# An attention block's third output product inside the attention loop, early splits of the first pair's operands, and a reordered first step

## The chip, the cores and the metric

One core of a Trainium2 chip runs the whole kernel. The time is device microseconds of one execution; before the change three runs gave a median of 809.31 us (808.28 to 810.48).

## What is computed

A transformer block on x of 2048 rows and 512 columns, cut here to what matters. The 2048 rows are four segments of 512 (s = 0 to 3); there are 32 heads of 16.

```python
h = layernorm(x) * (1 + ca) + sa
q, k, v = h @ wq, h @ wk, h @ wv
for s in range(4):                       # per head
    p = softmax(q[s] @ k[s].T / 4 + causal)
    o[s] = g * mem_read(q[s]) + (1 - g) * (p @ v[s])
x = x + ga * (o @ wo)                    # the output products, one per segment
h = layernorm(x) * (1 + cb) + sb
x = x + gb * (gelu(h @ w1 + b1) @ w2 + b2)
```

## The kernel before, in words

Each large product is made of three fp32r matmuls: operands are split into a high and a low part (a rounded copy, then a subtract), and high x high, high x low and low x high are summed in PSUM.

**Stages.** First come q, k, v and the memory reads. Then the attention loop runs over P = 0 to 63, a pair of heads each; two P are a group Q, four P a unit U (8 heads, one slice g of a segment's o). S parts (L609) compute scores for the row maximum, which DVE takes (L616); the maxima go through a small transpose into `ms` on ACT (L129) and by a DMA into rows 96 to 98 of qst; T parts (L698) recompute the scores transposed with the maximum inside, ACT takes the exponential (L713, L724), POOL masks (L701), and PE multiplies by V (L738) into one bank `pv`, in a loop four P behind S. `pv_out` stores through ts to TD; `pv_in` reads the denominators dn and the products opk back; `den` (L773) stores reciprocals to RD, `rb_in` reads them back as rbB; `mix` (L787, L789), `o_hi` (oh) and `o_lo` (ol, L804) follow.

**What sets the order.** Two tables in PRM: 'order' lays S, T and the slots c0 to c9 within a P, and the other entries give positions (10 x P + slot) for everything else. DVE, ACT, POOL and PE each run in the order of the code, and so does SP, which issues nearly all DMAs. Each DMA on SP waits there for what it needs.

**Output products.** `wo_part(s, b, g)` (L815) adds slice g to rows b (128 of them) of segment s: three matmuls, so 12 for a block b and 48 for a segment. `wo_out` (L832) adds x and stores to X2D. Segments 0 and 1 do this inside the loop, in the bank `mm`, one block per group, at positions PRM['wo']; segments 2 and 3 do it after the loop, in the banks that the attention has left.

**The second half** runs in pairs of segments, p = 0 for segments 0 and 1, p = 1 for 2 and 3. `ln2_load`, `ln2_stats` (L564), `ln2_rstd` (crs, L150), `ln2_apply` (L571) and `ln2_turn` (transposes L577, hr L579) make hr. Seven operands, b11, b21, t1, t2, t3, t4 and b22, are hr tiles or differences of them (`r_sub`), split by `r_hi` and `r_lo` into R. A step `quad(n)` multiplies each by its part of w1 (six matmuls, `prod`, L1036), collects in the banks X, Y and V_, and stores gelu results s to GD; fourteen steps, seven per p. Products t4 and b22 of a step run inside the next one (`c21`, `c12`). Weights are loaded as `wa` (L839), combined as wb (`w_sub`), and split by `w_hi` (L1022) and `w_lo` (L1026). `bg(n, i, ...)` hangs work behind point i of step n. After seven steps the second product with w2 (L1320) follows.

Between loop and steps stands a hand-written stretch: the 48 matmuls of segment 2, four at a time around the transposes of segment 1, then segment 3's 48, with all splits of the first step's operands woven in, and what is left of units 14 and 15 called by `rest`.

Of the kernel before, what the change touches and what calls it, by code (L numbers as in the profile page):

```python
# [12 lines left out]
ALU = mybir.AluOpType  # L13
# [10 lines left out]
VROW = 560  # L24
# [26 lines left out]
 'wo': [[2, 10, 10, 10], [6, 10, 11, 11]],  # L51
 'woout': [10, 11],
# [4 lines left out]
 'ln': [[312, 339, 374, 408], [590, 618, 630, 636]],  # L57
# [26 lines left out]
 'wout': ['vvvv', 'vava', 'vvvv'],  # L84
# [5 lines left out]
 'wsub': [642, 650],  # L90
# [13 lines left out]
def block_kernel(ctx: ExitStack, tc: tile.TileContext, x, wq, wk, wv, wo, betaq, betam,  # L104
# [88 lines left out]
    vstack = ExitStack()  # L193
    vp = vstack.enter_context(tc.tile_pool(name="vp", bufs=1, side="right"))
    V = [vp.tile([128, VROW], F32, name=f"V{b}") for b in range(NB)]
# [355 lines left out]
    def ln2_load(s, tiles=None):  # L551
        if tiles:
            xt2[s] = tiles
            for b in range(4):
                sp.dma_start(tiles[b], X2D[s][:, b, :])
        else:
            t = ce.tile([128, 4, D], F32, tag="xt2", name=f"xt2_{s}")
            xt2[s] = [t[:, b, :] for b in range(4)]
            sp.dma_start(t, X2D[s])
# [27 lines left out]
    with ExitStack() as pb:  # L587
# [208 lines left out]
        def o_hi(U):  # L796
            oh = so.tile([128, 512], F32R, tag="oh", bufs=7, name=f"oh{U}")
            copy(PRM["ohe"], oh, opks[U])
            OHL[U] = oh

        def o_lo(U):
            ol = so.tile([128, 512], F32R, tag="ol", bufs=7, name=f"ol{U}")
# [6 lines left out]
        def wo_part(s, b, g):  # L809
            if g == 0 and s < 2:  # L810
# [9 lines left out]
        def wo_x(s, b):  # L820
            xbs[s, b] = so.tile([128, D], F32, tag="xb", bufs=4, name=f"xb{s}_{b}")
# [30 lines left out]

        NP = 64
# [8 lines left out]
        def wo_load(k):  # L862
            wors[k] = so.tile([128, D], F32, tag="xb", bufs=4, name=f"wor{k}")
# [51 lines left out]
        for s in range(NSEG - 1):  # L915
            for b in range(4):
                e = 160 * s + 230 + 20 * b
                ap(e + PRM["wox"][s], wo_x, s, b)
                if s < 2:
# [19 lines left out]
        for i, (ln, ld) in enumerate(zip(PRM["ln"], PRM["lnd"])):  # L939
            ap(ln[0], ln2_load, i)  # L940
            for b in range(4):
                ap(ln[1] + ld[0] * b, ln2_stats, i, b)
# [24 lines left out]
    vstack.close()  # L967

# [10 lines left out]
    with ExitStack() as pc:  # L979
        c1 = pc.enter_context(tc.tile_pool(name="c1", bufs=1, side="right", reuse_waits="tile"))  # L980
        pf = pc.enter_context(tc.tile_pool(name="psF", bufs=1, space=PSUM, reuse_waits="tile"))
        spare = pf.tile([128, 512], F32, name="spare")
        bx, by, bv = [[pf.tile([128, 512], F32, name=f"{n}{i}") for i in range(2)] for n in ("bx", "by", "bv")]
        PROD = ("b11", "b21", "t2", "t1", "t3", "t4", "b22")

        R = {n: [[c1.tile([128, 512], F32R, name=f"r{n}{i}{k}") for k in range(2)] for i in "hl"] for n in PROD}
# [4 lines left out]

        def hk(p, n):
            a, b = 2 * p, 2 * p + 1
# [409 lines left out]
```

## Time and profile before

| what | value |
|---|---|
| median of three runs | 809.31 us |
| the profiled execution | 810.6 us, span 808.9 us |
| PE busy | 782.7 us, 97% |
| DVE, ACT, POOL busy | 69%, 58%, 40% |
| mean granted PE clock | 0.996 |
| PE busy from 460 to 480 us, the end of the attention loop | 13.04 of 20 us, clock 0.90 |
| masked maxima (L616), 384 | 192.5 us on DVE, 553 ns each |
| exponentials (L713), 256 | 125.9 us on ACT, 557 ns each |

Busy time is what an engine's instructions span. Matmuls overlap one another, so a busy PE says only that one is always under way; how fast they follow is read from their starts. The number in square brackets behind a row of the timeline is the idle time of that engine ahead of it, with what ended it.

### The profile page before, as it was taken

The page shows a single profiled execution, that of the slowest core. Times are in us where ns is not written, and L with a number is a line of the kernel's source. Part 1 is how long each engine was busy: PE and PEld are TensorE (multiplying, and loading weights), DVE is VectorE, ACT ScalarE, POOL GpSimd, SP SyncE. Part 2 cuts the span into 40 slices and gives each one's busy share as a digit, 9 for nine tenths or more (in the row PEclk, how much of TensorE's full clock was granted, in tenths as well). Part 3 has the DMA queues.
Part 4 walks back from the last instruction along what each step waited for, and adds up shares of the span by engine and source line. Part 5 has one row for each costly group of instructions (what it writes and reads, how often), then busy time and mean ns, then how long its engine had stood idle before and what let it go on. Part 6 is the DMA issues. An engine that isn't in the chain of part 4 may idle for free.

```text
span 808.9 us, 14151 instructions
## 1 busy us (share of the span) xinstructions
PE 782.7 (97%) x4585; PEld 531.5 (66%) x4585; DVE 555.5 (69%) x1413; ACT 467.2 (58%) x914; POOL 327.0 (40%) x550
## 2 busy tenths in 40 slices
PE   8999999999999999999999879999999999999998
PEld 4877777866444455445544338778877888888886
DVE  6686697459888877896688567976668766532423
ACT  3465545465778766776688755677644336653221
POOL 1357366441478555677866641234000404300000
PEclk9999999999999999999999989999999999999999
DMA  9596857495565676766667744764665634445443
GB/s 336 176 315 230 290 182 234 146 339 154 154 192 171 177 199 175 220 212 189 185 182 205 213 132 132 243 206 137 221 233 183 200 127 155 158 143 169 158 135 112
DMA packets 107523, 156.10 MB, mean 193 GB/s; under 512 B 16181, under 2 KB 55477, under 8 KB 107065
## 3 DMA queue, kind: packets, MB, share of 16 engines
q1 hardware_dynamic: 104952, 153.23, 59.5%
q10 hardware_dynamic: 2496, 1.97, 0.8%
q8 instruction: 36, 0.59, 0.3%
q14 instruction: 39, 0.31, 0.1%
HBM read 93.95 MB, written 60.83 MB: 191 GB/s over the span
## 4 chain that ended last, share of the span: by engine, by line
PE 73%; DVE 7%; DMA 7%; ACT 5%; issue 3%; POOL 3%; SPq 1%; ACTq 0%; DVEq 0%; POOLq 0%
PE bx L1036 8%; PE pv L738 7%; PE att L698 6%; PE att L609 5%; PE q L315 5%; PE bx L1320 4%; PE k L315 4%; PE bv L1036 4%; PE by L1320 4%; PE bv L1320 4%; PE v L466 3%; PE mm L815 2%; PE spare L1320 2%; PE by L1036 2%; DMA RD<-dn 1%
## 5 line engine op out<-in xcount | busy, mean ns | idle before, releaser
L616 DVE CUSTOM_DVE_ANT_0 dump<-att,maskb 128x512 bf16<-128x512 f32 (+2 forms) x384 | 192.5, 553 | 22.5 <-PE att L609 19.8
L713 ACT ACTIVATE pt<-att 128x512 f32<-128x512 f32 (+1 forms) x256 | 125.9, 557 | 42.2 <-PE att L698 40.9
L701 POOL TENSOR_SCALAR_AFFINE_SELECT pt<-pt 128x256 f32<-128x256 f32 x256 | 100.9, 411 | 79.7 <-ACT pt L713 48.0
L698 PE MATMUL att<-qst,kst 99*128 99x512 bf16 (+3 forms) x512 | 107.9, 302 | 9.2 <-DMA qst<-ms 4.0
L609 PE MATMUL att<-kst,qst 96*128 96x512 bf16 (+2 forms) x384 | 94.2, 326 | 0.7 <-DVE nm L616 0.2
L851 POOL TENSOR_TENSOR wb<-wa 128x256 f32<-128x256 f32 x24 | 22.8, 950 | 162.6 <-DMA wa<-in_w 162.6
L738 PE MATMUL pv<-pt,V 128*32 128x512 f32 (+2 forms) x992 | 88.1, 446 | 0.0
L698 PEld LDWEIGHTS <-kst 99*128 99x128 bf16 x512 | 43.2, 97 | 62.1 <-issue 41.6
L138 DVE TENSOR_TENSOR gl<-s,gh 128x512 fp32r<-128x512 f32 x52 | 36.7, 706 | 66.9 <-ACT gh L135 66.9
L135 ACT ACTIVATE gh<-s 128x512 fp32r<-128x512 f32 x52 | 32.4, 629 | 74.8 <-PE spare L1320 31.7
L724 ACT ACTIVATE pt<-att 128x512 f32<-128x512 f32 (+1 forms) x128 | 56.9, 509 | 21.7 <-PE att L609 19.6
L609 PEld LDWEIGHTS <-qst 96*128 96x128 bf16 x384 | 33.1, 98 | 39.7 <-issue 23.8
L738 PEld LDWEIGHTS pv<-pt,V 128*32 128x32 f32 x992 | 22.1, 108 | 36.3 <-issue 25.7
L1041 ACT ACTIVATE s<-s,b1t 128x512 f32<-128x512 f32 x42 | 30.3, 721 | 20.1 <-DVE s L1045 19.9
L620 DVE TENSOR_REDUCE nm<-att 128x2 f32<-128x256 f32 x64 | 27.2, 426 | 21.0 <-PE att L656 18.5
L1045 DVE TENSOR_TENSOR s<-bv,s 128x512 f32<-128x512 f32 x28 | 19.2, 687 | 29.4 <-PE bv L1036 25.0
L616 DVE DVE_READ_ACCUMULATOR2_ANT nm<- 128x1 f32 x384 | 32.0, 83 | 0.0
L511 POOL TENSOR_TENSOR q<-qr,q 128x512 bf16<-128x512 f32 x16 | 18.6, 1165 | 27.9 <-ACT q L510 27.6
L502 POOL TENSOR_SCALAR qp<-qp 128x512 f32<-128x512 f32 x12 | 19.2, 1598 | 24.0 <-ACT qp L497 24.0
L1320 PE MATMUL bx<-w2h,gl 128*128 128x512 f32 (+1 forms) x70 | 26.6, 380 | 0.5 <-DVE gl L138 0.5
L1320 PE MATMUL bx<-w2h,gh 128*128 128x512 f32 (+1 forms) x70 | 26.0, 372 | 0.6 <-ACT gh L135 0.6
L315 PE MATMUL q<-Ahh,wqh 128*128 128x512 f32 x64 | 25.9, 405 | 0.2 <-DVE Ahh L137 0.2
(329 smaller groups left out, 2044.3 us busy)
## 6 DMA issues: line engine op xcount, KB each, us to landing
GD<-s SPq DMA_DIRECT2D x56, 256.0 KB
s<-GD SPq DMA_DIRECT2D x52, 256.0 KB
kst<-KD SPq DMA_DIRECT2D x32, 384.0 KB
qst<-QD SPq DMA_DIRECT2D x32, 384.0 KB
TD<-ts SPq DMA_DIRECT2D x32, 256.0 KB
wa<-in_w SPq DMA_DIRECT2D x28, 256.0 KB
QD<-q SPq DMA_DIRECT2D x16, 384.0 KB
KD<-k SPq DMA_DIRECT2D x16, 384.0 KB
```

What stands on the lines that cost most here:

```text
L135: act.activation(hi, src, AF.Copy)
L138: lo_eng.tensor_tensor(out=lo, in0=src, in1=hi.bitcast(F32), op=ALU.subtract)
L315: pe.matmul(ps, a[:, k, 128 * g:128 * g + 128], b[k], start=(k == 0 and i == 0), stop=(k == KB - 1 and i == 2))
L609: pe.matmul(ps, q_of(P, h, i), k_of(P, h, 128 * (i + 1)), start=True, stop=True)
L616: v.tensor_tensor_reduce(out=dump[n_dump[0] % 2][:, :n], in0=src, in1=maskb[:, 512 - n:], scale=-1.0, scalar=-4 * NEG, op0=ALU.add, op1=AL ...
L698: pe.matmul(ps, k[:99, e, 128 * j:128 * j + 128], q[:99, e, 128 * j:512], start=True, stop=True)
L701: pool.affine_select(out=t, in_=t, pattern=pattern, compare_op=ALU.is_ge, fill=0.0, base=0, channel_multiplier=-1)
L713: act.activation(pt[:, h, :], ps[:, :n], AF.Exp, scale=0.25)
L724: act.activation(pt, pv_, AF.Exp, scale=0.25)
L738: pe.matmul(ps[32 * c:32 * c + 32, lo:hi], V[4 * s + j][:, VW * hd:VW * hd + 32], pt[:, c % 2, lo - o:hi - o], start=start, stop=stop)
L1036: pe.matmul(ps, a[:, i, k, :], b[k], start=start and k == 0 and c == 0, stop=k == 1 and c == 2, skip_group_check=not start)
L1320: pe.matmul(ps, a[:, c], w[:, lo:hi], start=(f == 0 and i == 0), stop=(last and i == 2))
```

## The change

1. Segment 2's output product goes into the loop like the first two, at positions 552 to 621 (P = 55 to 62), in the bank `mm`; its blocks 1 and 3 leave through ACT and POOL, 0 and 2 through DVE. The two tags oh and ol keep 5 buffers, not 7, xb 3, not 4.
2. Segment 1's layernorm is loaded as four DMAs from P = 54 on, not as one at P = 59; its statistics come from 604 on, not 618, crs at 626, the application at 632.
3. The first pair's b11 and b21 are split inside the loop (positions 605 to 622) with DVE for both parts. Their tiles, and those of t1 and t3, take the storage of V tiles that are no longer read; V's rows grow from 560 to 576, and its pool stays open to the end.
4. After the loop the transposes of segment 1 come first, in the banks bx, then 24 matmuls of segment 3 (units 12 and 13), then the first step. Unit 14's 12 matmuls come behind the step's t2 product, unit 15's 12 inside the second step, with `close_wo`. In the first step t1's product runs ahead of t2's. t2 is formed as b22 - t1 in two tiles of its own, so b22 stays and is split later; t3, t4, b22's low part and two of the weights' low parts move into the step.
5. Y uses one bank per pair, not two in turn; segment 3's X2D is loaded in step 2, not 1. The ring gx has 4 tiles, not 6; every third pair of g parts goes to two weight tiles instead.

```diff
-VROW = 560
+VROW = 576
- 'wo': [[2, 10, 10, 10], [6, 10, 11, 11]],
- 'woout': [10, 11],
+ 'wo': [[2, 10, 10, 10], [6, 10, 11, 11], [2, 10, 10, 11]],
+ 'woout': [10, 11, 11],
- 'ln': [[312, 339, 374, 408], [590, 618, 630, 636]],
+ 'ln': [[312, 339, 374, 408], [548, 604, 626, 632]],
+ 'lnl': 15,
- 'wout': ['vvvv', 'vava', 'vvvv'],
+ 'wout': ['vvvv', 'vava', 'vava'],
- 'wsub': [642, 650],
+ 'wsub': [646, 652],
+ 'early': [605, 618],
...
+        RAW = {"t1": "b11", "t2": "b22", "t3": "b12", "t4": "b21"}
+        T2 = []
+        def raw(p, n):
+            return T2 if n == "t2" and p == 0 else hk(p, RAW.get(n, n))
...
+        def r_alloc(n, pl=None):
+            R[n] = [[pl.tile([128, 512], F32R, name=f"r{n}{i}{k}") if pl else
+                     vp.tile([128, VROW], F32R, tag="V", bufs=NB, name=f"r{n}{i}{k}")[:, :512] for k in range(2)]
+                    for i in "hl"]
...
+        for n, d in zip(("b11", "b21"), PRM["early"]):
+            ap(d, r_alloc, n)
+            ap(d, r_hi, 0, n, "v")
+            ap(d + 4, r_lo, 0, n)
...
-            X, Y, V_, t2 = bx[n % 2], by[n % 2], bv[n % 2], s2[n % 2]
+            X, Y, V_, t2 = bx[n % 2], by[n // FH], bv[n % 2], s2[n % 2]
...
+            if n == 0:
+                prod(n, "t1", V_, True)
...
+        for i in range(KB):
+            ln2_turn(1, i, bx[i % 2])
+            if i < 2:
+                w_hi(0, i)
+                w_lo(0, i)
+            if i == 1:
+                r_sub(0, "t1")
         for b in range(4):
             wo_seg(3, b, range(2))
...
-        bg(0, 1, ln2_load, 2)
-        bg(0, 2, close_wo)
-        bg(0, 4, r_sub, 0, "t4")
+        bg(0, 1, r_hi, 0, "t3")
+        bg(0, 2, r_lo, 0, "t3")
+        bg(0, 2, r_sub, 0, "t4")
+        bg(0, 3, wo_late, 2, 3)
+        bg(0, 3, r_lo, 0, "b22")
+        bg(0, 4, late_o)
         bg(0, 5, r_hi, 0, "t4")
         bg(0, 6, r_lo, 0, "t4")
+        for i in range(2, 4):
+            bg(0, 6, w_lo, 0, i)
+        bg(0, 6, ln2_load, 2)
+        bg(1, 2, close_wo)
```

Line numbers shift by a few in the changed kernel: output matmuls are L816, scores L699, transposes L578, the steps' matmuls L1057, w_lo L1047.

PE at the start of P = 62, before: the last scores of P = 61 (tiles kst_1838), then directly the first of P = 62 (kst_2076), which read the row maxima.

```order
L698 LDWEIGHTS kst_1838
L698 MATMUL att_2064<-qst_1837,kst_1838 128x128
L698 LDWEIGHTS kst_2076
L698 MATMUL att_2065<-qst_2075,kst_2076 128x512
L698 LDWEIGHTS kst_2076
L698 MATMUL att_2066<-qst_2075,kst_2076 128x512
```

The same place in the changed kernel, where the tiles of P = 61 and 62 are kst_2076 and kst_2139; woh and wol are the parts of wo, oh and ol those of o.

```order
L699 MATMUL att_2064<-qst_2075,kst_2076 128x128
L816 MATMUL mm<-woh,oh_4972 128x512
L816 MATMUL mm<-woh,ol_4974 128x512
L816 MATMUL mm<-wol,oh_4972 128x512
L816 MATMUL mm<-woh,oh_5209 128x512
L816 MATMUL mm<-woh,ol_5211 128x512
L816 MATMUL mm<-wol,oh_5209 128x512
L816 MATMUL mm<-woh,oh_5454 128x512
L816 MATMUL mm<-woh,ol_5456 128x512
L816 MATMUL mm<-wol,oh_5454 128x512
L699 LDWEIGHTS kst_2139
L699 MATMUL att_2065<-qst_2138,kst_2139 128x512
```

Nine matmuls of segment 2's last block stand between the two, in the bank mm.

PE right after the last product with V (into att_2065), before: segment 2's first block, with its twelve matmuls, then one group of transposes.

```order
L738 MATMUL att_2065<-pt_2_5847,V_209 32x256 x2
L738 MATMUL att_2065<-pt_2_5889,V_209 32x256 x2
L815 MATMUL bx_5953<-woh,oh_4713 128x512
L815 MATMUL bx_5953<-woh,ol_4715 128x512
L815 MATMUL bx_5953<-wol,oh_4713 128x512
L815 MATMUL bx_5953<-woh,oh_4969 128x512
```

The same place in the changed kernel: four groups of transposes in turn into two banks, then segment 3's first block.

```order
L739 MATMUL att_2065<-pt_2_5931,V_209 32x256 x2
L739 MATMUL att_2065<-pt_2_5973,V_209 32x256 x2
L578 MATMUL bx_6054<-ident,xt_1_5431 128x128 x4
L578 MATMUL bx_6055<-ident,xt_1_5431 128x128 x4
L578 MATMUL bx_6054<-ident,xt_1_5431 128x128 x4
L578 MATMUL bx_6055<-ident,xt_1_5431 128x128 x4
L816 MATMUL bv_6059<-woh,oh_5723 128x512
L816 MATMUL bv_6059<-woh,ol_5768 128x512
```

The 48 matmuls of segment 2 that stood here are gone, and the transposes, which stood one group behind each twelve of them, now follow one another.

DVE ahead of the first step's t4 product, before: w1tl are low parts of the weights that t4 and b22 use (w1tl_5992 in the first step), rt3l and rt4l low parts of the operands, xb the fourth output product's adds; the low part of t4 comes nine rows further on.

```order
L1010 TENSOR_TENSOR rt1l_5973<-hr_0_5028,rt1h_5971 128x512
L1010 TENSOR_TENSOR rt1l_5974<-hr_1_5145,rt1h_5972 128x512
L1026 TENSOR_TENSOR w1tl_5992<-wa_5608,w1th_5991 128x256
L1026 TENSOR_TENSOR w1tl_5992<-wb_5904,w1th_5991 128x256
L1010 TENSOR_TENSOR rt3l_5977<-hr_0_6028,rt3h_5975 128x512
L1010 TENSOR_TENSOR rt3l_5978<-hr_1_6057,rt3h_5976 128x512
L1045 TENSOR_TENSOR s_5995<-by_5955,s_5995 128x512
L1026 TENSOR_TENSOR w1ml_5990<-wa_5731,w1mh_5989 128x512
L832 TENSOR_TENSOR xb_0_6093<-bx_5954,xb_0_6093 128x512
```

DVE ahead of the same product in the changed kernel: opk and ol belong to unit 15, w1tl_6065 is the first step's.

```order
L887 TENSOR_TENSOR rb22l_6051<-hr_2_6103,rb22h_6049 128x512
L887 TENSOR_TENSOR rb22l_6052<-hr_3_6109,rb22h_6050 128x512
L1047 TENSOR_TENSOR w1ml_6063<-wb_6009,w1mh_6062 128x768
L788 TENSOR_TENSOR opk_6075<-opk_6075,rbB_6153 128x512
L790 TENSOR_TENSOR opk_6075<-opk_6075,amB_6077 128x512
L805 TENSOR_TENSOR ol_6233<-opk_6075,oh_6231 128x512
L1047 TENSOR_TENSOR w1tl_6067<-wa_5770,w1th_6066 128x256
L1047 TENSOR_TENSOR w1tl_6067<-wb_6009,w1th_6066 128x256
L887 TENSOR_TENSOR rt4l_6047<-hr_2_5268,rt4h_6045 128x512
L887 TENSOR_TENSOR rt4l_6048<-hr_3_5387,rt4h_6046 128x512
L1047 TENSOR_TENSOR w1tl_6065<-wa_5632,w1th_6064 128x256
L1047 TENSOR_TENSOR w1tl_6065<-wb_5995,w1th_6064 128x256
```

The first step's w1tl stood ahead of the low part of t3 and now stand behind t4's; unit 15's mix and split, which ran ahead of the first step, stand ahead of t4's low part, and the four xb adds come six rows after the last row shown. The SP load of the third step's weights, wa_6186, is issued in the code at point 1 of the first step in both kernels, ahead of its first store to GD; it overwrites wa_5632, which the first of the two w1tl_6065 rows reads.

More of the change, by code (lines that the diff above doesn't have):

```diff
@@ L191, in block_kernel @@
                        base=0, channel_multiplier=-1)
-    vstack = ExitStack()
-    vp = vstack.enter_context(tc.tile_pool(name="vp", bufs=1, side="right"))
-    V = [vp.tile([128, VROW], F32, name=f"V{b}") for b in range(NB)]
+    vstack = ctx
+    vp = vstack.enter_context(tc.tile_pool(name="vp", bufs=1, side="right", reuse_waits="tile"))
+    V = [vp.tile([128, VROW], F32, tag="V", bufs=NB, name=f"V{b}") for b in range(NB)]
     hstack = ExitStack()
@@ L1152, in block_kernel, with late_o, wo_late @@
         r_sub(0, "t3")
[L1153 to L1166 removed]
+        for b in range(4):
+            wo_x(3, b)
+        def late_o():
+            rest(15, "mem_mix", "mix", "o_hi", "o_lo")
+            assert not left, left
+        def wo_late(lo, hi):
+            for b in range(4):
+                wo_seg(3, b, range(lo, hi))
         def close_wo():
+            wo_late(3, 4)
             for b in range(4):
```

131 lines of the change are left out of this document (49 added, 82 removed).

## The prediction, made before the changed kernel had run

> **What bounds the kernel now.** I read the page's shares first, then twenty-microsecond windows. TensorE (PE) is busy in 97% of the span, and the chain of work that ended last is 73% PE.
>
> ```profile
> PE 782.7 (97%) x4585; PEld 531.5 (66%) x4585; DVE 555.5 (69%) x1413; ACT 467.2 (58%) x914; POOL 327.0 (40%) x550
> ...
> PE 73%; DVE 7%; DMA 7%; ACT 5%; issue 3%; POOL 3%; SPq 1%; ACTq 0%; DVEq 0%; POOLq 0%
> ```
>
> The windows (stretch, its length, busy time of PE, PEld, DVE, ACT, POOL, granted clock, DMA share, GB/s) show one hole: the end of the attention stage.
>
> ```profile
> 420.00:440.00 20.00, 20.00 (x183) 9.73 (x180) 17.76 (x67) 16.72 (x38) 14.21 (x29) 1.00 0.67 193
> ...
> 460.00:480.00 20.00, 13.04 (x106) 4.44 (x102) 7.19 (x15) 12.40 (x29) 12.50 (x24) 0.90 0.63 192
> ```
>
> In the full stretches more PE work means more time; in the hole it is free. So the question is how many of the 48 moved matmuls (third product, four blocks of 12) land in the hole. The hole also has two stretches at half clock, each behind a PE gap:
>
> ```profile
> 465.00:469.00 4.00, 1.06 (x13) 0.42 (x6) 1.64 (x4) 2.75 (x7) 1.97 (x6) 1.00 0.65 203
> 469.00:472.40 3.40, 3.40 (x14) 0.70 (x13) 0.00 (x0) 1.50 (x4) 0.41 (x1) 0.51 0.41 125
> ...
> 477.00:479.00 2.00, 0.00 (x0) 0.00 (x0) 0.88 (x2) 0.84 (x3) 1.97 (x4) 1.00 0.87 282
> 479.40:482.60 3.20, 3.20 (x26) 1.55 (x20) 3.13 (x7) 0.00 (x0) 1.96 (x3) 0.50 0.22 70
> ```
>
> The chain in order of time tells why the last attention products come at 479: a small store (RD) and its read-back (rbB) hold a mix on VectorE (DVE), which is first in first out; the layernorm statistics behind it come late, the crs pair on GpSimd (POOL) later still, and the last masks (L701) wait behind crs.
>
> ```profile
> 462.09 6.81 DMA RD<-dn
> 468.96 3.93 DMA rbB<-RD
> 473.01 0.87 DVE opk L787
> ...
> 476.38 0.58 POOL crs L150
> 477.03 1.05 POOL crs L151
> 478.08 0.93 POOL pt L701 x2
> 479.06 4.04 PE att L738 x22
> ```
>
> **Term 1, blocks inside the full loop: +5.4 us.** The loop runs over 64 pairs of heads; ScalarE (ACT) copies ms once per group of two pairs, so these rows count groups.
>
> ```profile
> 287.39 0.27 ACT L129 ACTIVATE ms<-mm 48x128 bf16<-48x128 f32 x1
> ...
> 329.05 0.27 ACT L129 ACTIVATE ms<-mm 48x128 bf16<-48x128 f32 x1
> ...
> 404.33 0.26 ACT L129 ACTIVATE ms<-mm 48x128 bf16<-48x128 f32 x1
> ...
> 436.41 0.27 ACT L129 ACTIVATE ms<-mm 48x128 bf16<-48x128 f32 x1
> ```
>
> Four groups with an output block each took 41.66 us (287.39 to 329.05), 10.4 a group; four without took 32.08, 8.0 a group. A block of 12 costs 2.4 us there. In the change the first two blocks (pairs 55 to 58) and three matmuls of the third (pair 59) stand in that region: 2 x 2.4 + 0.6 = 5.4. One matmul of this kind takes 0.227 us from start to start, 42 of them from 497.38 to 506.92:
>
> ```profile
> 497.38 0.39 PE L815 MATMUL by<-woh,oh 128*128 128x512 f32 x1
> ...
> 506.92 0.39 PE L1036 MATMUL bx<-rb11h,w1mh 128*128 128x512 f32 x1
> ```
>
> So the ends are 0 (all hidden, against the rows) and 27 x 0.227 = 6.1 plus the copies of one block, about 8; I take 5.4, which rows of the same work show.
>
> **Term 2, the hole: -5.0 us.** The other 21 matmuls (4.8 us) stand in pairs 60 to 62, nine of them right ahead of pair 62's first scores, where PE now waits for the DMA of ms:
>
> ```profile
> 462.47 0.23 PE L677 MATMUL mm<-identb,nm 128*128 128x128 bf16 x1 [1.59 <-POOL nm L672]
> ...
> 468.84 1.19 PE L698 MATMUL att<-qst,kst 99*128 99x512 bf16 x3 [2.94 <-DMA qst<-ms]
> ```
>
> They fill 1.59 and 2.94, so I cost them at nothing: pair 62 starts at 468.7 as now, but without the 2.94 gap ahead of it. If that cover goes (ms landing sooner), they cost up to 2 us and the landing gives it back. From there ACT sets the pace:
>
> ```profile
> 469.38 1.47 ACT L713 ACTIVATE pt<-att 128x512 f32<-128x512 f32 x3 [1.64 <-PE att L698]
> 472.36 0.49 ACT L713 ACTIVATE pt<-att 128x384 f32<-128x384 f32 x1 [1.51 <-PE att L698]
> ...
> 476.95 0.90 ACT L724 ACTIVATE pt<-att 128x512 f32<-128x512 f32 x2
> ```
>
> At full clock its 1.51 stall goes, with the 0.60 for oh further on: last exponential at about 475.7 instead of 477.85. The statistics now stand ahead of the mix, so crs comes before pair 62's last masks, not before pair 63's. Last mask about 476.4, last product 477.3 to 479; I take 478.0 against 483.03, minus 5.0. What is late next is ACT. Ends: 0 (the DMA as late and both cuts back) and -6.5.
>
> New in the hole is DVE work: four casts and four subtracts of the early split, put at 0.6 each, 4.8 us, in a stretch where DVE is busy 7.19 of 20. Queued behind them are three of the statistics, the mix and, on its result, oh on ACT; by the RD rows the mix waits till 468 or later anyway, so nothing. Two queues get a wait: SP's store of the third block waits for DVE's add ahead of RD, and the last block's for POOL's add ahead of the dn read; both adds run before the next DMA would issue now (462.09 and, by the chain of dn behind rbB, after 468.96).
>
> [...]
>
> ```profile
> 480.94 1.27 POOL L794 TENSOR_TENSOR amB<-amB,rm 128x512 f32<-128x512 f32 x1 [0.85 <-DMA rm<-rdd]
> ...
> 481.12 1.12 DVE L774 TENSOR_SCALAR dn<-dn,omg 128x32 f32<-128x32 f32 x1
> ...
> 490.27 0.24 DVE L774 TENSOR_SCALAR dn<-dn,omg 128x32 f32<-128x32 f32 x1
> ```
>
> If the eight splits hold up POOL's masks so that half of their 4.8 us shows, term 2 is -2.6.
>
> **Term 3, from the last attention product to the end of the first step: -8.6 us.** Before, from 483.03 to the end of the first step's t4 product is 37.1 us, with PE waiting 1.78 at t4:
>
> ```profile
> 517.95 0.50 PE L1036 MATMUL bx<-rt4h,w1th 128*128 128x512 f32 x1 [1.33 <-ACT s L1096]
> ...
> 519.14 0.50 PE L1036 MATMUL bx<-rt4l,w1th 128*128 128x512 f32 x1 [0.45 <-DVE rt4l L1010]
> ```
>
> After, PE's own work up to t4 with all 48 matmuls of the fourth output product is 10.9, eight products of six 10.9, transposes 1.5: 23.3. But PE waits. The third and fourth transposes need ACT's hr of the first and second, with the w_hi copies between (0.68, 0.52, 0.68 from start to start): 1.7 us.
>
> ```profile
> 486.55 0.78 ACT L579 ACTIVATE hr<-mm,cols 128x512 f32<-128x512 f32 x1 [1.72 <-PE mm L577]
> 487.23 0.62 ACT L1022 ACTIVATE w1mh<-wa 128x512 fp32r<-128x512 f32 x1
> 487.75 0.83 ACT L1022 ACTIVATE w1mh<-wb 128x768 fp32r<-128x768 f32 x1
> ```
>
> And DVE, not PE, sets t4. It was busy 31.04 us up to t4's low part; a 128x512 operation takes 0.60 from start to start:
>
> ```profile
> 483.03:519.14 36.11, 31.04 (x52) 1.00 0.55 182
> ...
> 491.29 0.68 DVE L832 TENSOR_TENSOR xb<-bx,xb 128x512 f32<-128x512 f32 x1
> 491.89 0.68 DVE L804 TENSOR_TENSOR ol<-opk,oh 128x512 fp32r<-128x512 f32 x1
> 492.49 1.29 DVE L1010 TENSOR_TENSOR rb21l<-hr,rb21h 128x512 fp32r<-128x512 f32 x2
> ```
>
> In the new order stand 18 subtracts (t1, t2, t3, t4, and the low parts of t1, t2, t3, t4, b22), two mixes of two, two ol, one add and two w_lo of that size, 27 x 0.60 = 16.2; two 768-wide w_lo, 1.8; four quarter w_lo, 1.4; den, 0.6: 20.0. It starts 2.0 after the last attention product (ts, hr, w_hi on ACT first), and waits for the second w_hi 0.9, for both oh copies 0.8 and for ACT's copies in the step 0.9: t4's low weights at 24.6, its end 25.8. The 2.7 of the last twelve output matmuls, now behind t4, still have to run: 28.5, against 37.1. Ends: 25.0 if DVE keeps up, 34 if DVE needs as long as the 31.04 of now.
>
> **Term 4, second step: +2.9.** SP issues DMAs in order. The load of the third step's weights (wa) overwrites what the w_lo now behind t4 read, so it waits till 24.6, and with it, behind it, the first store of GD. ACT copies the second step's s1 only when that store is done, and PE's second t2 needs the copy. Before, 6.6 us lay between issue and copy:
>
> ```profile
> 511.66 0.34 SPq L1042 DMA_DIRECT2D GD<-s  x1
> ...
> 518.30 0.60 ACT L1072 ACTIVATE s<-bx 128x512 f32<-128x512 f32 x1 [0.41 <-DMA GD<-s]
> ```
>
> Then a 1 MB load stood ahead of it and 1 MB of stores behind, which is not so now. Bounds 2 and 6.6, and I take 4.0, since the read-back above took 3.93: issue 26.0, landed 30.0, copied 30.6, where PE is ready at 28.5: 2.2. The last 0.7 is t1: its bank is freed by the fourth product's first add, which on DVE stands behind a statistic that waits for a load. VROW, fewer buffers for oh, ol and xb, and gx 4 with two borrowed tiles cost nothing: the borrowed pair is dead once the last step that reads it has done its first two products, three pairs stay, and each oh or xb is free a pair of heads or more before its next writer.
>
> **Sum:** +5.4 - 5.0 - 8.6 + 2.9 = -5.3, so 810.6 (span 808.9 and 1.7 around it) becomes 805.3 for the profiled execution. That one lay 1.3 above the median of the runs shown, 809.31, so I predict 804.
>
> **The rivals.** *More:* DVE keeps ahead of t4 (term 3 -12.1): 800.5; against it, the 31.04. *The clock stays cut:* the trace shows the clock halved right behind PE gaps of 2.94 and at least 2.0 (none of PE from 477 to 479). [...] Each would take half of 3.4 us, 1.7, and term 2 is -1.6: 807.4. *The masks are blocked*, as above: 806.4. *A wash:* pair 62 begins and ends as now, because the small DMAs still take 6.81 and 3.93, and the loop takes all of 6.1: -5.3 + 5.0 + 0.7 = +0.4, 809.7. This is also the case in which the change only moves work about. *Slower:* SP's queue and slow DMAs. With the 6.6 of before, s1's copy comes 2.6 later than I take; the loads of stage 2, behind it in the queue, hold DVE's statistic and the adds behind it, so t1 waits about 3.0 and not 0.7; and as the same slow DMAs bring ms late, term 2 falls to -2.0: -5.3 + 2.6 + 2.3 + 3.0 = +2.6, 812. It decides from some 6 us per store or load on; for it speaks that the RD row shows 6.81, against it that a megabyte fewer is queued ahead, both there and here.
>
> **How the numbers follow.** Forecast 804: 0.42; more: 0.13; masks: 0.08; clock cut: 0.07; wash: 0.13; slower: 0.17. A difference of 0.3% (2.4 us) is about what a measurement of this kernel tells from none: below 806.9 lie the first three, 0.63; within it the next two, 0.20; above 811.7, 0.17. The range goes from 798, past "more" towards -6.5 and -12.1 together (797 without the 2.2), up to 811, short of the slower case.
>
> **What would show it.** Right: groups with the third product's blocks take 10.4; no gap over 1 us ahead of pair 62's scores and full clock from 469 to 483 on the old scale; the last attention product at about 483 as before, with the third product done; from it to t4's end about 26, with PE waiting two to three for DVE's w_lo or low part. Wrong: a clock of 0.5 in the hole, masks half as long again as now, PE waiting over 4 us for s1 in the second step, or groups above 11.

## The result and the profile after

| | before | changed kernel |
|---|---|---|
| median, 20 runs each | 810.58 us (807.1 to 813.3) | 805.45 us (801.9 to 809.6) |
| ratio | | 0.9942, 95% interval 0.9924 to 0.996 |
| the profiled execution | 810.6, span 808.9 | 809.1, span 807.4 |

The forecast was 804, or -5.3 us between profiles; the medians differ by 5.1. The profiled execution of the changed kernel is one of its slowest, 3.7 above its median, so the two profiles differ by only 1.5. Cut at the same points of the program, they give (all from starts of rows; the "last attention product" ends 0.27 after its last start):

| stretch | before | after | difference | forecast |
|---|---|---|---|---|
| start to the copy of ms that read 436.41 before | 436.4 | 439.5 | +3.1 | 0 |
| two groups, with the first two blocks | 16.7 | 20.8 | +4.1 | +5.4 |
| from there to the last attention product | 29.9 | 25.4 | -4.4 | -5.0 |
| to the second step's t2 (t4 done, and all 48 matmuls of segment 3) | 37.2 | 29.4 | -7.8 | -8.6 |
| to the third step's t3 | 16.5 | 19.3 | +2.8 | +2.9 |
| to the end | 272.2 | 272.9 | +0.7 | 0 |
| sum | 808.9 | 807.4 | -1.5 | -5.3 |

The forecast column gives each term the row of its subject. Of term 4's +2.9, 2.2 stood for a wait of PE ahead of the second step's t2, and that point ends the row before; by these cuts the forecast was -6.4 and then +0.7. The ratios here and below leave out an execution that lay over 1.5% above the fastest of its kernel, which is one in all, of xb_dve, at 813.85 us.

PE's busy time and its share of the chain of work that ended last, on the page of the changed kernel:

```profile
PE 783.4 (97%) x4585; PEld 531.3 (66%) x4585; DVE 555.8 (69%) x1415; ACT 465.4 (58%) x912; POOL 329.2 (41%) x552
...
PE 77%; DVE 6%; ACT 6%; POOL 4%; DMA 3%; issue 3%; SPq 0%; ACTq 0%; DVEq 0%; POOLq 0%
```

DMA was 7% of that chain and is 3%: RD and its read-back have left it. In the windows of twenty microseconds the hole is full:

```profile
460.00:480.00 20.00, 20.00 (x165) 10.03 (x163) 15.74 (x39) 15.07 (x35) 15.76 (x25) 1.00 0.66 202
```

Before, PE was busy 13.04 of these 20, at a mean clock of 0.90.

**The groups.** The copies of ms on ScalarE, one per group of two pairs, in the changed kernel:

```profile
439.48 0.27 ACT L131 ACTIVATE ms<-mm 48x128 bf16<-48x128 f32 x1
449.90 0.27 ACT L131 ACTIVATE ms<-mm 48x128 bf16<-48x128 f32 x1
460.32 0.27 ACT L131 ACTIVATE ms<-mm 48x128 bf16<-48x128 f32 x1
469.94 0.26 ACT L131 ACTIVATE ms<-mm 48x128 bf16<-48x128 f32 x1
```

10.42, 10.42 and 9.62, where before (436.41, 444.87, 453.11, 462.74) they took 8.46, 8.24 and 9.63. The first two blocks cost 2.0 and 2.2, the third nothing: it fills what was a wait.

**The end of the loop.** The chain in order of time, in the changed kernel:

```profile
473.58 2.15 PE mm L816 x9
...
475.76 0.61 ACT xo L831
...
476.44 1.79 POOL xb L832
478.22 1.62 POOL pt L702 x2
...
480.14 1.05 POOL crs L153
481.19 2.28 POOL pt L702 x4
```

No DMA stands in it. GpSimd's queue does: its add for the last block, masks, the crs pair, masks. The last attention products on PE wait for it:

```profile
475.56 0.77 PE L699 MATMUL att<-qst,kst 99*128 99x512 bf16 x3
...
483.51 2.35 PE L739 MATMUL att<-pt,V 128*32 128x512 f32 x28 [1.73 <-POOL pt L702]
```

The 28 take 2.35, against 4.04 before at half clock.

**The stretch behind the loop.** PE's waits there:

```profile
487.31 0.66 PE L578 MATMUL bx<-ident,xt 128*128 128x128 f32 x4 [0.43 <-ACT hr L580]
488.50 0.66 PE L578 MATMUL bx<-ident,xt 128*128 128x128 f32 x4 [0.53 <-ACT hr L580]
...
499.54 0.50 PE L1057 MATMUL bx<-rt2h,w1mh 128*128 128x512 f32 x1 [0.81 <-ACT s L1093]
...
509.99 0.50 PE L1057 MATMUL bx<-rt4h,w1th 128*128 128x512 f32 x1 [1.97 <-ACT s L1120]
511.11 0.50 PE L1057 MATMUL bx<-rt4h,w1tl 128*128 128x512 f32 x1 [0.61 <-DVE w1tl L1047]
```

The wait of 1.97 is put down to ScalarE's copy of s3, but that copy stands behind the cast of t4, which stands behind the copy of oh, and oh waited for VectorE's mix. VectorE was busy 24.28 of the 26.60 us up to t4's end:

```profile
485.79:512.39 26.60, 22.23 (x102) 17.33 (x101) 24.28 (x42) 17.36 (x30) 3.06 (x2) 1.00 0.42 130
```

**The second and third step.** SP's load of weights and the store of GD, ScalarE's copy that waits for the store, and the third step's transposes:

```profile
509.24 0.93 SPq L841 DMA_DIRECT2D wa<-in_w  x2
510.21 0.51 SPq L1063 DMA_DIRECT2D GD<-s  x1
...
513.69 0.60 ACT L1093 ACTIVATE s<-bx 128x512 f32<-128x512 f32 x1 [3.75 <-DMA GD<-s]
...
527.78 1.69 PE L578 MATMUL mm<-ident,xt 128*128 128x128 f32 x4 [1.24 <-DVE xt L572]
```

PE gets to the second step's t2 at 515.13, after s1's copy, and waits for nothing there. The loss is in the third step: 1.24 for the layernorm's application (0.34 before), and then, in windows, a stretch at half clock that the third step did not have before:

```profile
526.87:530.28 3.41, 2.12 (x9) 1.37 (x10) 2.22 (x5) 2.58 (x6) 0.00 (x0) 1.00 0.97 258
530.28:533.69 3.41, 3.41 (x12) 2.72 (x11) 2.39 (x3) 1.86 (x5) 3.23 (x4) 0.50 0.83 231
```

### The profile page after: what moved, and what is told of

Its sections match the earlier page's. It is cut to its first block, busy times and chain, and to the rows that moved or that the text cites. A ratio compares the mean times of both kernels' runs of the same rounds, so it can differ in the third digit from the quotient of the medians.

```text
span 807.4 us, 14166 instructions
## 1 busy us (share of the span) xinstructions
PE 783.4 (97%) x4585; PEld 531.3 (66%) x4585; DVE 555.8 (69%) x1415; ACT 465.4 (58%) x912; POOL 329.2 (41%) x552
## 3 DMA queue, kind: packets, MB, share of 16 engines
q10 hardware_dynamic: 2496, 1.97, 0.8%
## 4 chain that ended last, share of the span: by engine, by line
PE 77%; DVE 6%; ACT 6%; POOL 4%; DMA 3%; issue 3%; SPq 0%; ACTq 0%; DVEq 0%; POOLq 0%
PE pv L739 8%; PE bx L1057 8%; PE att L699 7%; PE att L610 6%; PE q L317 5%; PE bx L1330 5%; PE bv L1057 4%; PE by L1330 4%; PE bv L1330 4%; PE k L317 4%; PE mm L816 4%; PE v L468 3%; PE spare L1330 2%; DMA qst<-ms 2%; PE by L1057 2%
## 5 line engine op out<-in xcount | busy, mean ns | idle before, releaser
L617 DVE CUSTOM_DVE_ANT_0 dump<-att,maskb 128x512 bf16<-128x512 f32 (+2 forms) x384 | 192.3, 553 | 28.2 <-PE att L610 26.2
L702 POOL TENSOR_SCALAR_AFFINE_SELECT pt<-pt 128x256 f32<-128x256 f32 x256 | 102.7, 419 | 82.1 <-ACT pt L714 51.2
L699 PE MATMUL att<-qst,kst 99*128 99x512 bf16 (+3 forms) x512 | 106.8, 301 | 6.7 <-DMA qst<-ms 3.3
L853 POOL TENSOR_TENSOR wb<-wa 128x256 f32<-128x256 f32 x24 | 20.6, 860 | 157.4 <-DMA wa<-in_w 79.4
L699 PEld LDWEIGHTS <-kst 99*128 99x128 bf16 x512 | 42.9, 97 | 59.6 <-issue 39.3
L140 DVE TENSOR_TENSOR gl<-s,gh 128x512 fp32r<-128x512 f32 x34 | 24.2, 712 | 46.0 <-ACT gh L137 43.8
L137 ACT ACTIVATE gh<-s 128x512 fp32r<-128x512 f32 x34 | 21.2, 628 | 48.9 <-PE spare L1330 20.8
L1066 DVE TENSOR_TENSOR s<-bv,s 128x512 f32<-128x512 f32 x28 | 19.2, 687 | 31.0 <-PE bv L1057 25.4
L513 POOL TENSOR_TENSOR q<-qr,q 128x512 bf16<-128x512 f32 x16 | 18.7, 1166 | 27.8 <-ACT q L512 27.6
L140 DVE TENSOR_TENSOR w1ml<-s,w1mh 128x512 fp32r<-128x512 f32 x18 | 13.0, 722 | 21.0 <-ACT w1mh L137 20.9
L137 ACT ACTIVATE w1mh<-s 128x512 fp32r<-128x512 f32 x18 | 11.3, 628 | 26.7 <-PE spare L1330 13.9
```

The lines of the kernel that those rows point to most:

```text
L137: act.activation(hi, src, AF.Copy)
L140: lo_eng.tensor_tensor(out=lo, in0=src, in1=hi.bitcast(F32), op=ALU.subtract)
L617: v.tensor_tensor_reduce(out=dump[n_dump[0] % 2][:, :n], in0=src, in1=maskb[:, 512 - n:], scale=-1.0, scalar=-4 * NEG, op0=ALU.add, op1=AL ...
L699: pe.matmul(ps, k[:99, e, 128 * j:128 * j + 128], q[:99, e, 128 * j:512], start=True, stop=True)
L702: pool.affine_select(out=t, in_=t, pattern=pattern, compare_op=ALU.is_ge, fill=0.0, base=0, channel_multiplier=-1)
```

## The experiments

Twelve kernels. Stretches are read from each profile: A is from VectorE's reduction for pair 55 to that for pair 62, B from there to the last attention product, C from there to t4's end, D to the second step's t2, E from the third step's first product to its t3. A ratio is to the time of before on the same chip, with its 95% interval; a kernel that ran once has none. The stretches are of one execution each.

| run | ratio | A | B | C | D | E |
|---|---|---|---|---|---|---|
| before | 1 | 28.2 | 30.1 | 37.2 | 37.2 | 11.1 |
| changed kernel | 0.9942 (0.9924 to 0.996) | 33.5 | 25.6 | 26.6 | 29.4 | 13.6 |
| third_alone | 1.0044 (1.0013 to 1.0075) | 33.5 | 30.8 | 35.3 | 36.2 | 10.9 |
| ln_alone | 0.9975 (0.9949 to 1.0002) | 34.7 | 24.0 | 35.9 | 36.4 | 11.1 |
| ln_split | 0.9983 (0.9951 to 1.0014) | 30.7 | 27.6 | 38.0 | 38.0 | 11.1 |
| late_split | 0.9948 (0.9925 to 0.997) | 33.6 | 25.2 | 29.2 | 31.9 | 13.8 |
| xb_dve | 0.9887 (0.9843 to 0.9931) | 32.7 | 25.3 | 25.8 | 30.1 | 10.7 |
| apply_first | 0.9904 (0.9874 to 0.9935) | 32.7 | 25.6 | 26.3 | 29.0 | 10.9 |
| filler | 0.9911 (0.9873 to 0.9949) | 32.7 | 25.6 | 27.5 | 30.5 | 11.5 |
| unit15_last | ran once | 32.7 | 27.4 | 23.2 | 34.3 | 9.9 |
| mix15_last | ran once | 33.2 | 25.6 | 23.3 | 28.1 | 11.1 |
| dve_twice | ran once | 32.7 | 25.7 | 27.9 | 32.4 | 10.4 |
| rm_dve | ran once | 33.4 | 25.7 | 27.1 | 30.4 | 11.3 |
| combo | 0.9854 (0.983 to 0.9878) | 36.9 | 25.0 | 23.2 | 27.5 | 10.0 |

### third_alone: only the third product's blocks, in the kernel before

```diff
- 'wo': [[2, 10, 10, 10], [6, 10, 11, 11]],
+ 'wo': [[2, 10, 10, 10], [6, 10, 11, 11], [2, 10, 10, 11]],
...
-        wo_seg(2, 0, range(4))
...
-        wo_out(2, 0)
```

Expected: 

> The kernel before, with one part of the change: segment 2's output product in the loop at the new positions, and its 48 matmuls and four adds gone from the stretch behind the loop, where nothing else changes its order. My theory: the blocks cost about 5.2 us up to pair 62, as in the changed kernel (S of pair 55 to S of pair 62: 33.5 against 28.2 before); the hole gives back 2 to 4.4, depending on whether the late statistics still hold the last masks; and from the last attention product to the end of t4, VectorE needs about as long as before less four adds of 0.6, so 37.1 becomes 33 to 34.5, though PE has 10.9 us less to do there. Sum: -0.5 to -3, so 0.996 to 0.999 of the time before. Rival, PE sets that stretch as well: 37.1 becomes about 27 to 29, and this kernel alone is 5 to 8 us faster than before, 0.990 to 0.994, at least as fast as the full change.

Measured: 0.4% slower than before, where 0.1 to 0.4% faster was expected. A is the 33.5 of the changed kernel, as expected. B gave nothing back, where 2 to 4.4 was expected, though the matmuls fill PE's gaps; the chain in order of time in this run still has the small DMAs and the statistics:

```profile
467.51 6.04 DMA RD<-dn
...
473.62 4.20 DMA rbB<-RD
...
481.75 1.05 POOL crs L151
482.81 0.93 POOL pt L701 x2
483.74 0.04 issue
483.78 4.38 PE att L738 x22
```

C fell by 1.9 only, to 35.3 (33 to 34.5 was expected), with 10.9 us less for PE. So PE's own work does not set that stretch, against the rival (27 to 29). That VectorE does isn't shown by this run: PE waited 6.56 there for ScalarE's hr, and its clock was one half from 491.28 to 501.52. The blocks alone are a loss.

### ln_alone and ln_split: only the layernorm's new place, in the kernel before

ln_alone keeps one load of 1 MB, ln_split has the change's four.

```diff
- 'ln': [[312, 339, 374, 408], [590, 618, 630, 636]],
+ 'ln': [[312, 339, 374, 408], [548, 604, 626, 632]],
```

Expected of the first: 

> The kernel before, with one part of the change: segment 1's layernorm is loaded at position 548 (in one DMA) and its statistics stand at 604 on, crs at 626, the application at 632; no block is moved. My theory: the statistics no longer stand behind the mix that waits for the read-back, crs no longer holds the last masks, and the last attention product comes 2 to 3 us sooner (S of pair 62 to last attention product 29.8 before, 27 to 28 here), with the waits of PE for the DMA of ms and the half clock still there. Behind the loop about half of it is kept, since VectorE sets that stretch: -1 to -2.5 in all, 0.997 to 0.999. Rival: the exponentials and not the statistics set the end, so nothing moves by more than 0.5 us.

Measured: B fell by 6.1 and A rose by 6.4, because in SP's queue a read of qst stood behind the 1 MB. Its row in the chain, and PE's wait:

```profile
442.94 10.81 DMA qst<-QD
```

```profile
453.80 1.03 PE L609 MATMUL att<-kst,qst 96*128 96x512 bf16 x2 [4.31 <-DMA qst<-QD]
```

That run tells little of the statistics, hence the second. Expected: 

> The kernel before, with segment 1's layernorm as in the change: four loads of 256 KB from position 548 on, 15 positions apart, statistics at 604, crs at 626, application at 632; no block is moved. The run with one load of 1 MB at 548 had a read of qst behind it in SP's queue that took 10.8 us, so it does not tell what the statistics' place is worth. My theory: their place alone closes the hole's end. S of pair 55 to S of pair 62 stays at 28 to 29 us, and from S of pair 62 to the last attention product 30.1 becomes 26 to 28; from there to t4's end it stays at 35 to 37. Sum -2 to -4, 0.995 to 0.9975 of the time before. Rival: the gaps of PE and the half clock set the end (then it takes the blocks to fill them), and it stays at 29.5 to 30.5.

Measured: B fell by 2.5, as expected, and A rose by 2.5, which was not: PE waits 1.34 in A for a read of qst, which shares its queue with the four loads; the rest of the 2.5 was not traced. The last products start 23.5 after pair 62's reduction, against 26.2 before and 23.4 in the changed kernel, but take 4.48 at half clock:

```profile
476.79 4.48 PE L738 MATMUL att<-pt,V 128*32 128x512 f32 x28 [3.06 <-POOL pt L701]
```

So B's -4.4 has two parts: the last products start 2.8 sooner after that reduction, and they run at full clock, 1.7 (2.35 for 4.04). What brings them forward this run can't tell any more than the first: pair 62's reduction came 2.5 later and the last products no sooner, 54.2 after pair 55's reduction, against 54.4 before. What holds them there is the mix itself: ScalarE waits 2.32 for it ahead of oh, and the last exponentials stand behind oh. Two kernels with A alike can. In third_alone (A 33.5), with the statistics behind the mix, the last products start 26.7 after the reduction, and in late_split (33.6), the next run, which has the statistics' new place and no early split, 23.0:

```profile
479.91 2.35 PE L739 MATMUL att<-pt,V 128*32 128x512 f32 x28 [1.28 <-POOL pt L702]
```

The two also differ in buffers and in the stretch behind the loop, so this is strong support and not a test of the one move. Neither part of the change has both gains alone.

### late_split: the early split undone

```diff
-            ap(d, r_hi, 0, n, "v")
-            ap(d + 4, r_lo, 0, n)
...
                 r_sub(0, "t1")
+        for n in ("b11", "b21"):
+            r_hi(0, n)
+            r_lo(0, n)
```

The split of b11 here comes behind t1's subtract, which has overwritten b11, so that product is of t1's numbers; the work is the same. Expected: 

> The changed kernel with the early split undone: b11 and b21 are split behind the transposes (casts on ScalarE, subtracts on VectorE), still in the storage of the V tiles. My theory, VectorE sets the stretch from the last attention product to t4's end: four subtracts of 0.6 more there, so t4 ends 2.4 later on that clock (26.6 becomes 29), perhaps 3 with the casts ahead of t1's on ScalarE, and the loop's end gives back at most 0.5: +2 to +3 us against the changed kernel, 0.997 of the time before. Rivals: PE or SP sets the stretch, then 0 to +0.5; or the splits were not free in the loop (they held masks there), then the loop ends 1 to 2 sooner and the sum is 0 to +1.

Measured: C is 2.6 longer, D 2.5, and the loop's end (A and B together) 0.3 shorter: VectorE sets the stretch, and the splits were all but free in the loop. PE's clock was one half in C from 498.73 to 502.14, but what PE waits for in t4, as in the changed kernel, is VectorE's low weight:

```profile
510.07 0.50 PE L1055 MATMUL bx<-rt4h,w1tl 128*128 128x512 f32 x1 [0.60 <-DVE w1tl L1045]
```

In the whole time the 2 to 3 us are not resolved (0.9948 and 0.9942, with overlapping intervals); the stretches carry the verdict.

### xb_dve: the last block's add on VectorE

```diff
- 'wout': ['vvvv', 'vava', 'vava'],
+ 'wout': ['vvvv', 'vava', 'vavv'],
```

Expected: 

> The changed kernel with one block's way out altered: the last block of segment 2 is added by VectorE straight from the bank, not by a ScalarE copy and a GpSimd add. My theory: in the changed kernel GpSimd's queue holds the last masks (its add of 1.79 us, then masks, the crs pair and six masks without a pause), so without the add the last attention product comes 1.3 to 1.8 us sooner and PE's wait of 1.73 ahead of it shrinks to 0.5 or less; the time falls by 1 to 1.8 us. Rival: the exponentials or VectorE's work end just as late, and nothing moves by more than 0.4 us.

Measured: the theory fell. The wait ahead of the last products went from 1.73 to 1.36 and B from 25.6 to 25.3; the exponentials come as late, and the crs pair is still ahead of the masks. The run is faster for another reason: in E nothing waited and no half clock came (10.7 for 13.6); PE was 0.7 later at D, behind a half clock from 506.58, and so the layernorm's application was in time for it. That is where the time went in the profile; that it was so in its other three executions isn't shown.

### apply_first and filler: what the half clock in the third step hangs on

```diff
-            for i in range(2):
-                bg(n, 8 + i, ln2_applies, s, 2 * i, 2 * i + 2)
+            bgs[n + 1, 1].insert(0, (ln2_applies, (s, 0, 4)))
```

Expected: 

> The changed kernel with one move on VectorE: the four applications of the layernorm of segment 2 (third step), and of segment 3 (fifth step), stand ahead of the weights' low part that waits for ScalarE, not behind it. My theory: PE's wait of 1.24 ahead of the third step's first transposes falls below 0.6, the window of 3.41 us then holds too little idle time to halve the clock, and from the third step's first product to its t3 product 13.6 us becomes 10.7 to 11.3: -2 to -2.8 us against the changed kernel. Rival: the half clock there has nothing to do with that wait, and only 0.7 to 1 goes; or the weights' low part comes late in its turn, and nothing goes.

Measured, as the theory had it: E is 10.9, with no half clock in it (in the whole time, 0.9904, the interval still overlaps that of the changed kernel), and the wait is

```profile
524.66 1.24 PE L578 MATMUL mm<-ident,xt 128*128 128x128 f32 x3 [0.45 <-DVE xt L572]
```

In the second the wait isn't shortened but filled:

```diff
+                if s == 2 and d == 0:
+                    bg(n, 10, prod, 2, "t2", mm, True)
                 bg(n, 10 + d, ln2_turn, s, d, (mm, spare)[d % 2])
```

Expected: 

> The changed kernel with work added that nobody reads: six matmuls of 128x512 (into the bank that the transposes overwrite next) ahead of the third step's first transposes, where PE waits 1.24 us. My theory, the clock is halved for a window of 3.41 us when PE has idled for about half of the window before: the six fill the wait, no half clock follows it, and from the third step's first product to its t3 product 13.6 us becomes 11.8 to 12.4, 1.3 to 1.8 us less although PE has 1.36 us more to do. Rival, the clock does not depend on a wait this short: 13.6 stays or grows by 0.1 to 1.4, with the half clock still there.

Measured: E is 11.5, a little below the forecast and 2.1 less than in the changed kernel, with 1.36 us of matmuls more and no wait of PE shown in it. The windows around the six have full clock:

```profile
527.36:530.78 3.42, 3.19 (x15) 2.29 (x15) 2.08 (x5) 2.60 (x5) 0.00 (x0) 1.00 0.89 248
530.78:534.19 3.41, 3.41 (x20) 2.84 (x20) 2.94 (x4) 2.53 (x5) 3.10 (x4) 1.00 0.86 273
```

### unit15_last and mix15_last: unit 15 behind the low weights

```diff
-        bg(0, 4, late_o)
...
             bg(0, 6, w_lo, 0, i)
+        bg(0, 6, late_o)
```

Expected: 

> The changed kernel with the mix and the split of unit 15 behind the first step's low weights on VectorE (and its copy on ScalarE behind s3's), not ahead of t4's split. My theory: t4 starts about 1.6 sooner and the twelve matmuls of unit 15 behind it wait for their operands instead, so from the last attention product to the second step's t2 29.4 becomes 28.6 to 29.0, since VectorE's work in all is the same. Rival: something else than VectorE's order holds t4, and nothing moves.

Measured: t4's end came 3.5 sooner, and the twelve matmuls then waited 5.85, so D was 34.3, not 28.6 to 29; it ran once, in 809.9, where before had a median of 812.4 on that chip. The edit had moved GpSimd's multiply as well, to behind four sums that wait for a load; the row of VectorE's mix:

```profile
513.84 0.69 DVE L790 TENSOR_TENSOR opk<-opk,amB 128x512 f32<-128x512 f32 x1 [5.36 <-POOL amB L795]
```

The second leaves that multiply in its place. Expected: 

> As unit15_last, but GpSimd's multiply for unit 15 keeps its old place, ahead of GpSimd's four weight sums of the third step, which wait for a load; in unit15_last it stood behind them, and the mix waited 5.36 us for it. Only the mix, the copy of oh and the subtract of ol stand behind the low weights. My theory: t4's end comes 2.5 to 3.5 sooner than in the changed kernel, the twelve matmuls follow with little waiting, and from the last attention product to the second step's t2 29.4 becomes 27.3 to 28.6. Rival: the twelve matmuls or s1 are as late as before, 29.0 or more.

Measured: C 23.3, D 28.1, inside the forecast. PE no longer waits at t4, so VectorE's list isn't what sets t4's end in this order. It ran once, in 801.2, where before had a median of 814.9 on that chip.

The two runs show one thing more. Their last attention products waited alike, and took 4.04 in unit15_last and 2.35 in mix15_last:

```profile
482.13 4.04 PE L739 MATMUL att<-pt,V 128*32 128x512 f32 x28 [1.75 <-POOL pt L702]
```

```profile
479.93 2.35 PE L739 MATMUL att<-pt,V 128*32 128x512 f32 x28 [1.73 <-POOL pt L702]
```

### dve_twice and rm_dve: is it VectorE, and what holds it?

```diff
         bg(0, 3, r_lo, 0, "b22")
+        bg(0, 3, r_lo, 0, "b22")
```

Expected: 

> The changed kernel with two subtracts doubled: the low part of b22 in the first step is made twice on VectorE (same result). My theory, VectorE sets the end of t4: its end, counted from the last attention product, comes 1.2 later, 26.6 becomes 27.6 to 28.0. Rival: ScalarE or PE sets it, then 26.4 to 26.9.

Measured: C is 27.9, in the range, but not for the reason given alone: the low weight that t4 waits for came only 0.4 later, and the rest is a half clock under t4's matmuls (0.43 from start to start from 510.10 on, 0.23 in the changed kernel). GpSimd's multiply for unit 15 ran here from 494.44, for 1.29, beside VectorE's 128x32 scaling, which took 0.96 (0.24 in the changed kernel), and was over before the pair of subtracts, which took 1.28 (2.38 in the changed kernel): 0.4 less in all, a part of the 1.2. Inconclusive by itself; late_split carries the point.

```diff
-                (pool if PRM["rme"] == "p" else v).tensor_tensor(out=am, in0=am,
+                (pool if PRM["rme"] == "p" and U < 15 else v).tensor_tensor(out=am, in0=am,
```

Expected: 

> The changed kernel with unit 15's multiply with rm (L795) on VectorE, ahead of the mix, not on GpSimd. In the changed kernel two subtracts on VectorE took 2.30 us from start to end of the second while this multiply ran on GpSimd, against 1.20 for other pairs. My theory, the two engines held each other up: the pair takes 1.2 and VectorE, with 0.6 more to do and 1.1 less to wait, is 0.3 to 0.6 earlier at t4's end. Rival: the 2.30 has another cause and stays, and t4's end comes 0.6 later.

Measured: the pair of subtracts, in the changed kernel and then in this run:

```profile
497.99 2.38 DVE L874 TENSOR_TENSOR hr<-hr,hr 128x512 f32<-128x512 f32 x2
```

```profile
498.62 1.29 DVE L874 TENSOR_TENSOR hr<-hr,hr 128x512 f32<-128x512 f32 x2
```

In the changed kernel GpSimd's multiply ran from 497.68, for 1.54; with it gone from GpSimd the pair on VectorE is 1.1 shorter. t4's low part then started 0.4 sooner, but t4 ended 0.5 later, because a half clock fell on it (from 511.22 to 514.63).

### combo: three of the moves together

Expected: 

> The changed kernel with three moves at once: the last block of segment 2 added by VectorE (as xb_dve), the mix of unit 15 behind the low weights (as mix15_last), and the layernorm's applications ahead of the weights' low part (as apply_first). My theory, from the runs so far: 0.8 in the loop's end, 1 to 2 in the stretch to the second step's t2, and 2.7 in the third step, less than their sum where one wait takes another's place: 0.986 to 0.990 of the time before, 3 to 6 us below the changed kernel. Rival: only the half clock of the third step was worth something, then 0.990 to 0.992 like apply_first.

Measured: 0.9854, a little more than forecast, and faster than before and than the changed kernel, with all five times between 802.1 and 804.1 where before stood at 814.9. D is the shortest of all runs, and C and E are within 0.1 of the shortest. A has a wait of 1.90 for a DMA of ms that took 7.14 and a half clock behind it (eight products with V took 1.74 there, 1.06 in the changed kernel), in the profiled execution.

## Why the prediction was right, and where not

The time (804 forecast, 805.45 measured), the sign and the size came out; the four terms each came within 1.3 us. That the sum came so close is in part luck, because errors cancel. Without the two half clocks of the profiled execution (1.7 each, at pair 35 and in the third step) the table would give, as an estimate, -7.0 for the four terms and +2.1 for what the sum did not have, together -4.9, where the medians differ by -5.1. By its steps:

- **Term 1**, +5.4: +4.1. The 10.4 a group was right to the row (10.42). A group without a block takes 8.2 to 8.5 just there, not 8.0, so a block costs 2.0 to 2.2; and the third block's first matmuls, put at 0.6, cost nothing.
- **Term 2**, -5.0: -4.4. The mechanism had a part too many. Filling PE's gaps gives nothing back by itself (third_alone: B 30.8). What counts is an earlier start of the last products (2.8), which goes with the statistics standing ahead of the mix, and the full clock under them (1.7); the second is luck in part, for unit15_last lost it again behind a wait as long. "What is late next is ACT" was half of it: GpSimd was late as well, with its add, the crs pair and six masks. The add had been booked at nothing; but taking it away brought only 0.4, since the exponentials are late too.
- **Term 3**, -8.6: -7.8. That PE's own work doesn't set the stretch is shown by third_alone (C 35.3 with 10.9 us less for PE), that VectorE does by late_split (+2.6 for the splits). PE waited 2.58 ahead of and in t4, where two to three were forecast. Too small was VectorE's list: it was busy 24.28, not 20.0 plus waits; five of the eight weight sums (L853) ran behind the last product and were not in it, and GpSimd's multiply cost 1.1.
- **Term 4**, +2.9: +2.8, but by another mechanism, so this number was luck. The forecast wait for s1 was 2.2 (by the sum's own times, copied at 30.6 and ready at 28.5, it is 2.1), and none came: the load left at 509.24, as soon as VectorE was done with a w1tl ahead of t4's low part, not behind t4's own low weights as had been predicted (by its time, it overwrites another buffer than the one named there); the store followed at 510.21, s1 was copied at 513.69, and PE came at 515.13. The cost came in the third step: the application of the layernorm was 0.9 later against PE, behind segment 3's adds, statistics and a low part of the weights, and the half clock behind it cost 1.7. apply_first took both away.
- **What the sum lacked**: +3.1 ahead of the blocks. Segment 0's layernorm is loaded in four DMAs too, and three of them now go out at once beside the DMA of ms, where the single one waited 2 us longer. SP's row and PE's, in the changed kernel:

```profile
329.05 2.25 SPq L560 DMA_DIRECT2D xt<-X2D  x4
```

```profile
335.19 0.60 PE L699 MATMUL att<-qst,kst 99*128 99x512 bf16 x2 [1.70 <-DMA qst<-ms]
```

From the reduction of pair 34 to that of pair 36 the kernels with one load took 8.3 to 8.5 (before, third_alone, ln_alone), the changed kernel and those made from it 9.0 to 9.6, and 10.8 to 11.0 in the three of them where a half clock followed. So 0.5 to 1 us, and 2.5 with the clock, were not in the sum. The four loads are at most a part of it: ln_split has them too, in the kernel before, and took 8.8. What adds the rest in the changed kernel is open, and so are 0.8 more in the group ahead of the copy of ms at 431.10 (8.9, before 8.1) and the +0.7 at the end. With the 3.1 the last attention product came at 485.75, not at about 483.

**The rivals.** The blocked masks did not come: the last six took 3.38, 0.56 each (before, four took 2.03, 0.51 each), and B kept 4.4 of 5.0. That half of the splits' 4.8 us would show was the author's estimate, and no run shows it. What did get longer fell elsewhere, on VectorE while GpSimd's multiply with rm ran: the pair of subtracts took 2.38 against 1.29 (changed kernel, rm_dve), and the 128x32 scaling 1.12 (481.12, in the kernel before) and 0.96 (dve_twice) against 0.24. The half clock did come back, at pair 35 (335.72 to 339.13) and in the third step (530.28 to 533.69) and not in the hole, in this execution. Slow DMAs did not decide: the store of GD took 3.5 from issue to the copy behind it.

## What to carry to other kernels

Moving matmuls into a hole helps when the thing that made the hole moves too: here the gaps were a symptom, and a read-back with the statistics queued behind it was, as far as these runs show, the cause. Behind it the next limit (VectorE's list of splits) pays or not, so add up that engine's whole list, with what other engines' instructions do to it (1.1 us here, for one multiply on GpSimd). And a wait on PE can be worth more than it lasts: the 1.24 us in the third step were followed by 3.41 us at half clock, 1.7 us of work, and E was 2.7 us shorter where the wait fell to 0.45 (apply_first) and 2.1 where matmuls that nobody reads filled it (filler).

## What the runs showed of the hardware

Between 180 and 790 us the granted clock went to one half four times in the two profiles of the main pair, for 3.41 us each: from 469.05 and 479.29 in the kernel before, from 335.72 and 530.28 in the changed kernel. The two starts lie 3 times 3.41 us apart in the one and 57 times in the other; in third_alone it stayed at one half for 10.24, as above. Some windows of that length, with PE's idle time in each (the ends of matmuls are modelled) and the granted clock in the window behind it:

| run | window | idle time of PE, us | clock behind it |
|---|---|---|---|
| before | 465.64 to 469.05 | 2.94 | 0.50 |
| before | 475.88 to 479.29 | 2.42 | 0.50 |
| rm_dve | 507.80 to 511.22 | 2.05 | 0.50 |
| unit15_last | 478.82 to 482.24 | 1.75 | 0.50 |
| changed kernel | 332.30 to 335.72 | 1.70 | 0.50 |
| changed kernel | 526.87 to 530.28 | 1.29 | 0.50 |
| changed kernel | 506.38 to 509.79 | 1.77 | 1.00 |
| mix15_last | 478.36 to 481.77 | 1.57 | 1.00 |
| before | 516.84 to 520.25 | 1.56 | 1.00 |
| before | 458.81 to 462.22 | 1.50 | 1.00 |
| changed kernel | 479.07 to 482.49 | 0.71 | 1.00 |
| filler | 527.36 to 530.78 | 0.23 | 1.00 |

The three rows with 2.05 and more were followed by half clock, the two with 0.71 and less were not, and between 1.29 and 1.77 both occurred; what decides there isn't shown. So a wait of 1.75 was followed by half clock and one of 1.73 was not, which is a difference of 1.7 (the pair of rows under mix15_last), and the changed kernel's times spread over 7.7 us. Its profiled execution held two such stretches behind short waits (1.70 and 1.24), worth 3.4 us in all, and lay 3.7 above the median; that its other executions differ by just this isn't shown.
